# Where the down products stand among the gate and up products: the empty places move to a unit's ends, and the last five units of a half give out two columns a place

## The chip, the core and the metric

The kernel runs on one core of a Trainium2 chip. The core has TensorE (matmuls, with a queue of its own for loading weights), VectorE, ScalarE, GpSimd and SyncE, each with one queue in which instructions start in their written order; they wait for each other through semaphores. In the profile they are PE and PEld, DVE, ACT, POOL and SP. The metric is the device time of one execution in microseconds (us).

## The reference, cut to what matters

```python
def reference(x, wqkv, w_phi, wo, w_gate, w_up, w_down):
    xn = layernorm(x)                       # x is [1, 2048, 576]
    s = hedgehog_attention(xn)              # 32 heads of 18, then @ wo
    g = silu(xn @ w_gate) * (xn @ w_up)     # [2048, 4608]
    return x + s * silu(g @ w_down)         # [1, 2048, 576]
```

The inputs are float32. The change is in the FFN, the third and fourth line: gate and up projections, their gated product, and the down projection.

## The kernel before, in words

The attention takes the first 460 us or so; it also lays out `xn` and its sums as operands for the FFN. The FFN takes the rest. It treats the 2048 rows in two halves of 1024 (`i` = 0 and 1), and in each half the 4608 hidden columns in 36 blocks of 128. One block of one half is a **unit**; `n` is its place in the half, 0 to 35. Five units of half 0 and four of half 1 were computed early and are loaded from memory (`stored`); the others run `gate_up`.

`gate_up` computes gate and up of a unit by Strassen's scheme with seven products. Each is 7 matmuls of 128 x 512, accumulating into PSUM tiles `px` (two buffers), `py` and `pw` (one each). One unit runs them in this order: `px` (A11), `pw` (S1), `py` (A12), `px` again (S2), `px` (S3), `px` (A22), `pw` (S4). Between them other engines read: ScalarE copies `px` into `yp` after the first (L813), takes a snapshot `s` of `px` after the fourth and the fifth (L788), and applies silu to `py` (L800) and `px` (L804); VectorE adds snapshots to `pw` (L793) and makes the two parts of the hidden block, `ha` (L809) and `hb` (L805). The next matmul into the same tile has to wait for these readers. The order of ScalarE's queue matters too: in half 0 each unit's weights are prepared on the fly, with casts on ScalarE (L60), splits on VectorE (L61) and sums on GpSimd (L744 to L747).

The down projection is put off and cut into **items**, which are given out at the four **places** of a unit, between the products. Groups of four units (two pairs) make seven down products `p1` to `p7`, again by Strassen's scheme, of two items each, and an item costs as many columns as it has pairs: two, and 12 matmuls of 128 x 288 into a `pd` tile, of which there are two. VectorE then adds `pd` to a sum in SBUF (L1030). Units 32 and 33 are a pair alone, whose fourteen items have one column, 6 matmuls. The last two units, 34 and 35, are done plainly (`plain`): eight items of 12 matmuls, for which ScalarE first fills `pd` (or `px`, `py`, `pw`) with the sums so far (L923). Before these, the seven sums have to be combined into four (`combine`, at no cost in columns): its first part comes after `p6` in the queue (L1059 and L1060 on VectorE, L1061 on GpSimd, L1062 and L1063 on VectorE), its second after `p3` (L1067 on GpSimd, L1068 on VectorE). The second half's plain items are followed by silu, the product with the attention's rows (L903), the addition of `x` (L906) and the store (L907).

The queue's rule is `fill`, called at each place. It gives out items until it has given `share` columns (2, or 3 in the last five units, so that two two-column items go out), and stops when no more than `LAG` = 3 columns wait. A group of four units brings 28 columns for 16 places, so in steady state two of the 16 places stay empty. The operations are then ordered by a scheduling layer from priorities and readiness, which may move a later product into an empty place; the order it settles on is fixed in the program.

Of the kernel before, what the change touches and what calls it, by code (L numbers as in the profile page):

```python
# [23 lines left out]
NF = F // P  # L24
# [7 lines left out]
FIRST = (EARLY + 1, EARLY)  # L32
TAILS = (NF - EARLY + 3) // 4
LAG = 3
RUSH = NF - 5
LN_EPS = 1e-5
DEN_EPS = 1e-6

# [10 lines left out]
def gated_hedgehog_kernel(ctx: ExitStack, tc, x, w_qk, w_v, w_phi, wo, w_gu, w_tail, w_down, ident_in, mask_in, out):  # L49
# [88 lines left out]
    with ExitStack() as att:  # L138
# [17 lines left out]
        with ExitStack() as wst:  # L156
# [4 lines left out]
            with ExitStack() as pst:  # L161
# [101 lines left out]
                last, rest, _ = norm_block(2, xns[0:4])  # L263
# [508 lines left out]
    def stored(src, fill):  # L772
# [5 lines left out]
        return h  # L778

    def gate_up(w, xo, fill, opening):  # L780
        A11, A12, A22, S2, S4, S3, S1 = xo
        xp, yp, wp = (fps.tile([P, BT], F32, name=n, bufs=b) for n, b in (("px", 2), ("py", 1), ("pw", 1)))
        h = h_tile()

        def snap(ps):
            t = short("s", 3)
            with tc.high_priority():
                snaps.append(nc.scalar.copy(t, ps))  # L788
            return t

        def add(ps, t):
            with tc.high_priority():
                nc.vector.tensor_add(t, ps, t)  # L793


        if opening == 0:
            nc.tensor.matmul(yp, w[0][0][:, 0], A11[0], start=True, stop=True)

        def silu_y():
            nc.scalar.activation(yp, yp, AF.Silu)  # L800

        def silu_x(s3):
            with tc.high_priority():
                tops.append(nc.scalar.activation(xp, xp, AF.Silu))  # L804
            nc.vector.tensor_mul(h[1], xp, s3)  # L805

        def top(s2):
            with tc.high_priority():
                anchor.append(nc.vector.tensor_mul(h[0], yp, s2))  # L809

        product(xp, w, 0, A11, True, False)
        with tc.high_priority():
            copies.append(nc.scalar.copy(yp, xp))  # L813
        product(wp, w, 4, S1, True, False)
        if opening < 2:
            product(xp, w, 5, S2, False, False)
            s2 = snap(xp)
            product(yp, w, 1, A12, False, True)
            silu_y()
            product(xp, w, 2, S3, False, False)  # L820
            s3 = snap(xp)
            add(wp, s3)
            add(wp, s2)
            zp = fps.tile([P, 2, 512], F32, name="pd", bufs=2)[:, 0]
            product(zp, w, 3, S4, True, True)
            add(zp, s2)
            top(s2)
            product(xp, w, 6, A22, False, True)
            silu_x(s3)
            return h  # L830
        fill()
        product(yp, w, 1, A12, False, True)
        silu_y()
        product(xp, w, 5, S2, False, False)
        s2 = snap(xp)
        fill()
        product(xp, w, 2, S3, False, False)
        s3 = snap(xp)
        add(wp, s3)
        fill()  # L840
        product(xp, w, 6, A22, False, True)
        silu_x(s3)
        product(wp, w, 3, S4, False, True)
        add(wp, s2)
        top(s2)
        fill()
        return h
# [225 lines left out]
    for i in range(2):  # L1073
# [3 lines left out]
        for f in range(FIRST[i]):  # L1077
            order.insert(4 * f + 1 - i, f)
        units += [(i, n, f) for n, f in enumerate(order)]
    queue, anchor, share = [], [], [2]  # L1080
    copies, snaps, tops = [], [], []

    def look():
# [6 lines left out]
                step[1]()  # L1090
                step[1] = None

    def fill(lag=LAG):
        done = 0
        while queue and done < share[0] and (sum(c for q in queue for c, _ in q[2]) > lag or not queue[0][0]):
            look()
            c, item = queue[0][2].pop(0)
            item()
            done += c
            if not queue[0][2]:  # L1100
                queue.pop(0)
# [13 lines left out]
    fps = ctx.enter_context(tc.tile_pool(name="fps", bufs=1, space=PSUM, reuse_waits="tile"))  # L1115
    finals, late = {}, list(range(HT))
    for i, n, f in units:
        share[0] = 2 if n < RUSH else 3
        if i == 1 and n == 0:
            xo = operands(1)  # L1120
        if f >= FIRST[i]:
            w = kept.pop() if i and kept else ready.pop(0)
            if (i, f) == (0, NF - 1):
                kept.append(w)
            if todo and (i, f) != (0, NF - 1):
                ready.append(gate_up_weights(*todo.pop(0)))
        h = stored(h_dram[i, f], fill) if f < FIRST[i] else gate_up(w, xo, fill, f - FIRST[0] + (NF if i else 0))
        if n % 2 == 0:
            g = {"f": (f, units[units.index((i, n, f)) + 1][2]), "h": [h]}
            if n % 4 == 0:  # L1130
                group = []
            if n < NF - 2:
                group.append(g)
        else:
            g["h"].append(h)
        if n >= NF - 2:
            if n % 2:
                plain(i, g["f"], g["h"], finals)
            continue
        if n >= NF - 4 or n % 4 > 1:  # L1140
            strassen(i, group, n % 2, n < 4)
        if n % 2 == 0:
            continue
        if i and n >= 15 and late:
            with tc.issue_after(anchor[-1].ins):
                late_finish(late.pop(0))
        if n == NF - 3:
            for k in range(2):
                queue.insert(len(queue) - 2 + 3 * k,
                             [0, None, [(0, lambda i=i, k=k: combine(i, k, finals))]])  # L1150
# [37 lines left out]
```

## Time and profile before

| what | value |
|---|---|
| median of 3 runs | 1599.25 us (1598.89 to 1599.63) |
| the profiled execution's own time | 1602.31 us |
| its span, first to last instruction | 1600.40 us |
| TensorE matmuls busy | 1586.0 us |
| VectorE, ScalarE, GpSimd busy | 1172.6, 719.5, 665.5 us |
| granted TensorE clock | 0.999 |

The span is divided by engine: busy time is the sum of the instructions' durations, so an engine can be busy and still wait often for short times. A row of the timeline is one group of equal instructions, with its start, its duration, its engine and line, and in brackets how long the engine stood idle before it and what ended that. Matmuls overlap: a new 128 x 512 matmul starts about every 0.23 us though each lasts 0.39, so the distance between the starts of two groups says how long TensorE took for one.

### The profile page before, as it was taken

How to read it: one execution, taken by the hardware profiler on the slowest of the kernel's cores; microseconds unless marked ns; L12 is line 12 of the kernel's file. 1: busy time of each engine (PE TensorE's matmuls, PEld its weight loads, DVE VectorE, ACT ScalarE, POOL GpSimd, SP SyncE). 2: the span in 40 equal slices, each digit the busy share in tenths (PEclk: the TensorE clock that was granted, in tenths of full speed). 3: DMA queues.
4: the chain of work that ended last, by engine and by line, in shares of the span. 5: the costliest groups of instructions: out<-in, count | busy, mean ns of one | idle time of the engine just before them, and what ended most of it. 6: DMA issues, size and time to landing. Idle time of an engine off the chain costs nothing.

```text
span 1600.4 us, 25376 instructions
## 1 busy us (share of the span) xinstructions
PE 1586.0 (99%) x9415; PEld 1422.6 (89%) x9415; DVE 1172.6 (73%) x1729; ACT 719.5 (45%) x1400; POOL 665.5 (42%) x714
## 2 busy tenths in 40 slices
PE   8999999999999999999999999999999999999998
PEld 6899998999988888988888888888888888888887
DVE  7777769999946778887777778635667667666577
ACT  5633345445335654445444444454343333333334
POOL 2676762434115535644545435223324324133133
PEclk9999999999999999999999999999999999999999
DMA  9622243435376454555545453965545565565545
GB/s 283 219 82 80 89 147 118 120 105 144 118 247 233 165 184 165 175 180 179 179 171 194 170 190 116 333 220 148 156 138 153 183 187 159 174 181 184 144 117 178
DMA packets 123180, 268.28 MB, mean 168 GB/s; under 512 B 12978, under 2 KB 54066, under 8 KB 121778
## 3 DMA queue, kind: packets, MB, share of 16 engines
q1 hardware_dynamic: 107612, 244.73, 46.8%
q0 software_dynamic: 3552, 12.59, 2.8%
q10 hardware_dynamic: 11894, 9.35, 1.8%
q8 instruction: 74, 1.21, 0.3%
q14 instruction: 48, 0.39, 0.1%
HBM read 167.53 MB, written 99.09 MB: 167 GB/s over the span
## 4 chain that ended last, share of the span: by engine, by line
PE 94%; DVE 3%; DMA 2%; ACT 1%; issue 1%; POOL 0%; SPq 0%; ACTq 0%; DVEq 0%; POOLq 0%
PE px L759 25%; PE pd L876 25%; PE pw L759 12%; PE p L94 7%; PE py L759 6%; PE pe L94 5%; PE p L652 4%; PE kvp L330 2%; PE pt L632 2%; PE vx L418 1%; PE pt L625 1%; PE vw L418 1%; PE tp L249 1%; DMA wst<-in_A_w_qk 1%; PE vx L94 1%; PE vy L94 1%
## 5 line engine op out<-in xcount | busy, mean ns | idle before, releaser
L876 PEld LDWEIGHTS pd<-dw,hh 128*128 128x128 f32 x3012 | 424.0, 188 | 22.0 <-ACT pd L923 1.5
L876 PE MATMUL pd<-dw,hh 128*128 128x288 f32 x3012 | 438.5, 295 | 1.1 <-ACT pd L923 0.7
L759 PE MATMUL px<-X,w 128*128 128x512 f32 x1512 | 386.5, 391 | 0.0
L759 PEld LDWEIGHTS px<-X,w 128*128 128x128 f32 x1512 | 274.6, 188 | 48.9 <-ACT s L788 2.3
L759 PE MATMUL pw<-X,w 128*128 128x512 f32 x744 | 190.8, 392 | 0.0
L759 PEld LDWEIGHTS pw<-X,w 128*128 128x128 f32 x744 | 138.7, 188 | 29.4
L793 DVE TENSOR_TENSOR s<-pw,s 128x512 f32<-128x512 f32 x126 | 86.5, 688 | 97.9 <-ACT s L788 87.6
L1030 DVE TENSOR_TENSOR acc<-pd,acc 128x576 f32<-128x576 f32 x128 | 96.3, 753 | 78.9 <-PE pd L876 78.4
L788 ACT COPY s<-px 128x512 f32<-128x512 f32 x126 | 73.7, 585 | 156.6 <-PE px L759 156.6
L61 DVE TENSOR_TENSOR hh<-ha,hh 128x512 fp32r<-128x512 f32 x140 | 110.1, 812 | 22.2 <-ACT hh L60 21.5
L60 ACT CAST hh<-ha 128x512 fp32r<-128x512 f32 x140 | 82.7, 620 | 87.7 <-PE pd L876 74.3
L1002 POOL TENSOR_TENSOR hb<-hb 128x512 f32<-128x512 f32 x34 | 46.9, 1381 | 160.3 <-DVE hb L805 160.0
L94 PE MATMUL pe<-X,wh 128*128 128x512 f32 x340 | 105.6, 398 | 2.0 <-ACT wh L64 2.0
L61 DVE TENSOR_TENSOR w<-ld,w 128x512 fp32r<-128x512 f32 (+1 forms) x96 | 79.8, 832 | 35.6 <-ACT w L60 33.5
L759 PE MATMUL px<-X,wt 128*128 128x512 f32 x252 | 98.1, 389 | 0.0
L759 PE MATMUL py<-X,w 128*128 128x512 f32 x378 | 97.0, 391 | 0.0
L989 POOL TENSOR_TENSOR h<-ha,hb 128x512 f32<-128x512 f32 x34 | 44.7, 1313 | 125.1 <-DVE ha L809 94.1
L1015 POOL TENSOR_TENSOR ha<-ha 128x512 f32<-128x512 f32 x34 | 52.6, 1563 | 96.0 <-DVE hh L61 96.0
L60 ACT CAST w<-ld 128x512 fp32r<-128x512 f32 (+1 forms) x96 | 52.5, 549 | 84.8 <-POOL ld L747 55.0
L813 ACT COPY py<-px 128x512 f32<-128x512 f32 x63 | 36.0, 572 | 103.4 <-PE px L759 78.9
L744 POOL TENSOR_TENSOR ts<-ld 128x256 f32<-128x256 f32 x32 | 27.3, 855 | 122.7 <-issue 66.7
L759 PEld LDWEIGHTS py<-X,w 128*128 128x128 f32 x378 | 67.8, 188 | 10.6
(286 smaller groups left out, 3237.4 us busy)
## 6 DMA issues: line engine op xcount, KB each, us to landing
w_dram<-w SPq DMA_DIRECT2D x90, 512.0 KB
w<-w_dram SPq DMA_DIRECT2D x90, 512.0 KB
wt<-t_dram SPq DMA_DIRECT2D x62, 336.0 KB
ld<-in_B_w_gu SPq DMA_DIRECT2D x32, 512.0 KB
rt<-in_B_w_down SPq DMA_DIRECT2D x33, 288.0 KB
rb<-in_B_w_down SPq DMA_DIRECT2D x33, 288.0 KB
w_dram<-w SPq DMA_DIRECT2D x30, 256.0 KB
w<-w_dram SPq DMA_DIRECT2D x30, 256.0 KB
```

The costliest lines, as they stand in the source:

```text
L60: nc.scalar.copy(hi, src)
L61: nc.vector.tensor_sub(lo, src, hi)
L94: last = nc.tensor.matmul(ps, l, r, start=n == 0, stop=n == len(pairs) - 1)
L652: nc.tensor.matmul(ps[:, 0:HALF], a[0:w, g, jc], bw[0:w, g, n], start=k == 0, stop=k == 3 * NG - 1)
L759: nc.tensor.matmul(ps, l, r, start=first and n == 0, stop=last and n == len(mm) - 1, skip_group_check=True)
L788: snaps.append(nc.scalar.copy(t, ps))
L793: nc.vector.tensor_add(t, ps, t)
L876: nc.tensor.matmul(ps, l, r, start=first and n == 0 and m == 0, stop=n == len(hs) - 1 and m == 2, skip_group_check=True)
L989: sub(s, g["h"][0][0], g["h"][0][1])
L1002: nc.gpsimd.tensor_add(a21, a21, g["h"][1][1])
L1015: sub(a12, a12, g["h"][0][0])
L1030: nc.vector.tensor_add(a2, pd[:, :, 0:HALF], a2)
```

## The change

What `fill` gives out at each place changes in three ways. A unit's first place is left empty when no more than 6 columns wait (`2 * LAG`), unless it is the last unit of a half. The share is 2 columns at all places but those of unit 34, where it is 3; in unit 35 the lag is 0, so that it gives out all that is left. And an item that costs nothing (a part of `combine`) is given out as soon as it is at the head of the queue.

```diff
-RUSH = NF - 5
 def gate_up(w, xo, fill, opening):
...
-        fill()
+        if waiting() > 2 * LAG or not rush[1]:
+            fill()
         product(yp, w, 1, A12, False, True)
...
-    queue, anchor, share = [], [], [2]
+    queue, anchor, rush = [], [], [2, LAG]
...
+    def waiting():
+        return sum(c for q in queue for c, _ in q[2])
+
-    def fill(lag=LAG):
+    def fill(lag=None):
+        lag = rush[1] if lag is None else lag
         done = 0
-        while queue and done < share[0] and (sum(c for q in queue for c, _ in q[2]) > lag or not queue[0][0]):
+        while queue and (not queue[0][0] or done < rush[0] and waiting() > lag):
             look()
...
     for i, n, f in units:
-        share[0] = 2 if n < RUSH else 3
+        rush[:] = 3 if n == NF - 2 else 2, 0 if n == NF - 1 else LAG
```

Columns given out at the four places, worked out from the two rules, where they differ:

| unit | before | after |
|---|---|---|
| 22, 26, 30 of half 0; 18, 22, 26, 30 of half 1 | 2 2 0 0 | 0 2 2 0 |
| 2 of half 1 | 2 2 0 0 | 0 2 0 0 |
| 31 of both | 4 4 0 0 | 2 2 2 2 |
| 32 of both | 4 4 4 4 | 2 2 2 2 |
| 33 of both | 4 3 0 0 | 2 2 2 2 |
| 34 of both | 3 3 3 1 | 4 3 3 3 |
| 35 of both | 0 0 0 0, three left over | 2 2 2 1 |
| 0 of half 1 (stored, two places) | 2 3 | 2 2 |

The changed program's line numbers are one lower from L36 to L830 (so L813 becomes L812) and the same from L832 to L1080. Three places of the program follow, as the scheduling layer ordered them.

TensorE in unit 22 of half 0, from its first product, before:

```order
L759 MATMUL px<-X_60,w_8156 128x512 x6
L759 MATMUL px<-X_60,wt_5183 128x512
L759 MATMUL pw<-X_5202,w_8165 128x512 x6
L759 MATMUL pw<-X_5202,wt_5183 128x512
L876 MATMUL pd<-dw,hh 128x288 x12
L759 MATMUL py<-X_61,w_8156 128x512 x6
L759 MATMUL py<-X_61,wt_5183 128x512
L759 MATMUL px<-X_5207,w_8165 128x512 x6
L759 MATMUL px<-X_5207,wt_5183 128x512
L876 MATMUL pd<-dw,hh 128x288 x12
```

and in the change:

```order
L758 MATMUL px<-X_60,w_8156 128x512 x6
L758 MATMUL px<-X_60,wt_5183 128x512
L758 MATMUL pw<-X_5202,w_8165 128x512 x6
L758 MATMUL pw<-X_5202,wt_5183 128x512
L758 MATMUL py<-X_61,w_8156 128x512 x6
L758 MATMUL py<-X_61,wt_5183 128x512
L758 MATMUL px<-X_5207,w_8165 128x512 x6
L758 MATMUL px<-X_5207,wt_5183 128x512
L876 MATMUL pd<-dw,hh 128x288 x12
L758 MATMUL px<-X_5212,w_8169 128x512 x6
L758 MATMUL px<-X_5212,wt_5183 128x512
L876 MATMUL pd<-dw,hh 128x288 x12
```

The item between `pw` and `py` is gone; one stands after the fifth product instead.

ScalarE at the same place, in the change (`w2` and `w1` are the next unit's weights, `ld` and `ts` their raw parts and sums from GpSimd, `py_8347` is this unit's `yp`):

```order
L59 CAST w2_8325<-ld_8322 128x2x256
L59 CAST w1_8342<-ld_8322 128x256
L812 COPY py_8347<-px_8346 128x512
L59 CAST w2_8334<-ts_8324 128x2x256
L799 ACTIVATE py_8347<-py_8347 128x512
```

The first three rows stand as they did before; only the rows behind them moved (the casts of the next items' `hh` and `dw`, which stood behind the copy, now follow `py`'s silu).

VectorE in the last unit of half 1, from L1059 on, before (`pd_15853`, `pd_15861` and `pd_15869` are the last three one-column items, of `p2` and `p3`; `s`, `hb` and `ha` belong to units 34 and 35):

```order
L1059 TENSOR_TENSOR X02_11072<-X02_11072 128x1152
L793 TENSOR_TENSOR s_15656<-pw_15583,s_15656 128x512
L805 TENSOR_TENSOR hb_15585<-px_15581,s_15702 128x512
L809 TENSOR_TENSOR ha_15584<-py_15582,s_15656 128x512
L1060 TENSOR_TENSOR sx_11129<-sx_11129,X02_11072 128x1152
L1030 TENSOR_TENSOR acc_5181<-pd_15765,acc_5181 128x576
L1062 TENSOR_TENSOR acc_5181<-sx_11129,acc_5181 128x1152
L1063 TENSOR_TENSOR acc_5181<-acc_5181,sx_11129 128x1152
L61 TENSOR_TENSOR hh_15847<-hb_15585,hh_15847 128x512
L1030 TENSOR_TENSOR acc_5181<-pd_15853,acc_5181 128x576
L61 TENSOR_TENSOR dw_15844<-ld_15838,dw_15844 128x576
L793 TENSOR_TENSOR s_15817<-pw_15775,s_15817 128x512
```

and in the change (`pd_15802` and `pd_15820` are the items of `p2`, `pd_15828` and `pd_15854` those of `p3`; `s`, `ha` and `hb` belong to unit 35):

```order
L1059 TENSOR_TENSOR X02_11072<-X02_11072 128x1152
L1030 TENSOR_TENSOR acc_5181<-pd_15802,acc_5181 128x576
L792 TENSOR_TENSOR s_15817<-pw_15725,s_15817 128x512
L1060 TENSOR_TENSOR sx_11129<-sx_11129,X02_11072 128x1152
L1030 TENSOR_TENSOR acc_5181<-pd_15820,acc_5181 128x576
L1062 TENSOR_TENSOR acc_5181<-sx_11129,acc_5181 128x1152
L792 TENSOR_TENSOR s_15781<-pw_15725,s_15781 128x512
L1063 TENSOR_TENSOR acc_5181<-acc_5181,sx_11129 128x1152
L808 TENSOR_TENSOR ha_15726<-py_15724,s_15781 128x512
L1030 TENSOR_TENSOR acc_5181<-pd_15828,acc_5181 128x576
L804 TENSOR_TENSOR hb_15727<-px_15723,s_15817 128x512
L1030 TENSOR_TENSOR acc_5181<-pd_15854,acc_5181 128x576
```

Before, L1059 stood among the last results of unit 34; now it stands in the middle of unit 35, behind the add of `p6`'s second item. After the rows shown come, in both programs, the rest of what the plain items need: in the change the split of a weight (`dw_15876`), L1068 and the low part of a hidden block (`hh_15882`), in this order. The end of half 0 has the same rows in the same order; there TensorE has `px`, `pw`, `py`, `px` of unit 1 of half 1 ahead of the plain items.

## The prediction

> **What bounds the kernel now.** I read the page first, then busy time by stretches of 50 us, then the waits of TensorE's two queues, then the timeline where they lie.
>
> From the page: busy time by engine, and the chain that ended last.
>
> ```profile
> PE 1586.0 (99%) x9415; PEld 1422.6 (89%) x9415; DVE 1172.6 (73%) x1729; ACT 719.5 (45%) x1400; POOL 665.5 (42%) x714
> PE 94%; DVE 3%; DMA 2%; ACT 1%; issue 1%; POOL 0%; SPq 0%; ACTq 0%; DVEq 0%; POOLq 0%
> ```
>
> TensorE is the bound: the change neither adds nor removes a matmul, so it can only move the time in which TensorE waits. What there is to win is small, as the stretches (PE, PEld, DVE, ACT, POOL busy) and the load queue's waits (total, times, longest) show:
>
> ```profile
> 750.00:800.00 50.00, 50.00 (x271) 43.79 (x270) 39.07 (x55) 24.02 (x49) 26.54 (x26) 1.00 0.50 175
> 1550.00:1600.00 50.00, 43.35 (x258) 38.61 (x256) 38.05 (x53) 22.90 (x45) 17.62 (x13) 0.99 0.51 174
> ...
> PEld px L759 <- ACT s L788: 2.3, 12, 0.2
> PEld pd L876 <- ACT pd L923: 1.5, 3, 0.7
> PEld pd L876 <- DVE X L1030: 1.0, 2, 0.8
> PEld pd L876 <- DVE acc L1030: 0.9, 4, 0.3
> ```
>
> The first wait is the one the change is about: `xp` may be written again only when ScalarE's `snap` has read it, and a place left empty there has no matmuls to cover that. The other three are waits for a `pd` bank, in the last five units and the tail. Together 2.3 + 1.5 + 1.0 + 0.9 = 5.7 us: the most the change can win in the FFN.
>
> The prices I use are in the timeline. First, unit 22 of half 0 and the same place of units 26 and 30:
>
> ```profile
> 781.20 0.39 PE L759 MATMUL pw<-X,wt 128*128 128x512 f32 x1
> 781.31 0.75 POOL L747 TENSOR_TENSOR ld<-ld,ts 128x256 f32<-128x256 f32 x1
> 781.42 1.75 PE L876 MATMUL pd<-dw,hh 128*128 128x288 f32 x12
> 782.09 0.41 ACT L60 CAST w<-ld 128x256 fp32r<-128x256 f32 x1 [4.83 <-POOL ld L747]
> 782.40 0.58 ACT L813 COPY py<-px 128x512 f32<-128x512 f32 x1
> 783.03 1.63 PE L759 MATMUL py<-X,w 128*128 128x512 f32 x6
> 784.73 1.52 PE L759 MATMUL px<-X,w 128*128 128x512 f32 x6
> 786.32 1.75 PE L876 MATMUL pd<-dw,hh 128*128 128x288 f32 x12
> ...
> 849.43 0.58 ACT L813 COPY py<-px 128x512 f32<-128x512 f32 x1
> 850.07 1.67 PE L759 MATMUL py<-X,w 128*128 128x512 f32 x6
> ...
> 916.49 0.58 ACT L813 COPY py<-px 128x512 f32<-128x512 f32 x1
> 917.12 1.65 PE L759 MATMUL py<-X,w 128*128 128x512 f32 x6
> ```
>
> (Columns: start, duration, engine and instruction, then the idle time before it and what ended it.) A product of 7 matmuls takes 786.32 - 784.73 = 1.59 us, a two-column item of 12 about 1.58. A wait that the cover nearly hides costs the six matmuls 1.63 instead of 1.52: 0.1 us.
>
> The tail of half 1:
>
> ```profile
> 1555.57 1.75 PE L876 MATMUL pd<-dw,hh 128*128 128x288 f32 x12
> 1556.57 1.55 DVE L1030 TENSOR_TENSOR acc<-pd,acc 128x576 f32<-128x576 f32 x2 [1.43 <-PE pd L876]
> ...
> 1568.83 2.67 POOL L1061 TENSOR_TENSOR X<-X,acc 128x1152 f32<-128x1152 f32 x1 [12.25 <-DVE sx L1060]
> 1569.33 3.38 DVE L1062 TENSOR_TENSOR acc<-sx,acc 128x1152 f32<-128x1152 f32 x1
> 1572.64 1.34 DVE L1063 TENSOR_TENSOR acc<-acc,sx 128x1152 f32<-128x1152 f32 x1
> 1573.91 0.68 DVE L61 TENSOR_TENSOR hh<-hb,hh 128x512 fp32r<-128x512 f32 x1
> 1574.51 0.74 DVE L1030 TENSOR_TENSOR acc<-pd,acc 128x576 f32<-128x576 f32 x1
> 1575.17 0.74 DVE L61 TENSOR_TENSOR dw<-ld,dw 128x576 fp32r<-128x576 f32 x1
> 1575.33 3.11 POOL L1067 TENSOR_TENSOR acc<-acc,X 128x1152 f32<-128x1152 f32 x1 [3.83 <-DVE acc L1030]
> 1575.84 0.68 DVE L793 TENSOR_TENSOR s<-pw,s 128x512 f32<-128x512 f32 x1
> 1576.44 0.74 DVE L1030 TENSOR_TENSOR acc<-pd,acc 128x576 f32<-128x576 f32 x1
> ...
> 1579.57 0.64 ACT L923 COPY pd<-acc 128x576 f32<-128x576 f32 x1
> 1580.26 1.86 PE L876 MATMUL pd<-dw,hh 128*128 128x288 f32 x12 [0.21 <-ACT pd L923]
> 1582.58 1.86 PE L876 MATMUL pd<-dw,hh 128*128 128x288 f32 x12 [0.46 <-ACT pd L923]
> 1582.97 1.35 DVE L1068 TENSOR_TENSOR acc<-acc,X 128x1152 f32<-128x1152 f32 x1
> 1585.87 3.37 PE L876 MATMUL pd<-dw,hh 128*128 128x288 f32 x24
> 1589.07 1.75 PE L876 MATMUL px<-dw,hh 128*128 128x288 f32 x12
> ```
>
> From start to start, VectorE's costs are 0.66 for an add out of `pd`, 0.67 for a wide split, 0.60 for an add out of `pw` or a narrow split, 1.27 for a 1152-wide add; a down matmul is (1589.07 - 1585.87) / 24 = 0.133. An add can start 1.0 us after its one-pair item's first matmul (1555.57, 1556.57). GpSimd's and VectorE's adds inside SBUF exclude each other: L1062 ended 1.21 after L1061 did, 3.38 long where L1063 took 1.34. L1067 began beside the split of 1575.17 and ended 2.53 after it: 2.55 alone. Adds with an operand in PSUM (1575.84, 1576.44) ran beside it at full speed.
>
> **The change, part by part.** *Waits that go.* Of the 5.7 us I take 4.5 as won (a 0.19 wait of the load queue holds the matmuls for only about 0.1), between 2 and 5.7. New bank waits come where three one-column items meet two banks, in units 34 and 35: some four per half at 0.1 to 0.25, 1.1 in all.
>
> *The first place of units 22, 26 and 30 of half 0.* Without the item, `py` follows `pw` directly and must wait for the copy L813 into `yp`. In half 0 that copy stands in ScalarE's queue behind the cast of `w1`, which waited 4.83 us for GpSimd's L747; the order of both queues up to there is unchanged. TensorE would be ready at 781.42, the copy ends at 782.98, and `py` can start at 783.03, as before: 1.6 us idle. What hid it was the item, which now comes later and costs its 1.58 again. The other two units show the same copy and the same `py`. 3 x 1.58 = 4.75. If GpSimd's chain were short this would be 0. In half 1 no such cast stands ahead, so I cost it at nothing there: the cover is the product `pw`, 1.59 against a 0.58 copy.
>
> *The last unit of a half: later combine.* Before, unit 34 gave out all but three columns, and the first combine ran under unit 35. Now unit 35 gives out 7, and the combine cannot begin before the second item of `p6`. I count from the unit's first matmul, with no waits on TensorE: `p6`'s item starts at 8.75, the last item, `p3`'s, at 16.70, and the plain items could start at 17.50. VectorE's queue after that `p6` item, in the order of the changed program: add 9.75 to 10.41, split 11.08, L1059 12.35, add 13.01, `wp` add 13.61, L1060 14.88, add 15.54. GpSimd's L1061 runs 14.95 to 17.62, so L1062 ends at 18.83. GpSimd's L1067 no longer waits for `p2` and follows at once, to 21.4; VectorE's `wp` add runs beside it, but L1063 has to wait: 22.6. Then `ha` 23.2, the add that frees the bank of the first plain item 23.85, `hb` 24.45, add 25.1, split 25.8, L1068 27.05, and the low part of `hh` that the plain items need 27.75.
>
> At the end of half 1 TensorE does 10 plain matmuls (written ahead as 3 + 2 + 3 + 2) and then stands until 27.8, where without waits it would have reached that point at 17.50 + 10 x 0.133 = 18.83: 9.0 us. ScalarE's silu now stands ahead of the next bank's filling: 0.5 more. The remaining 86 matmuls and the output follow as before.
>
> The combine also issues loads: its rows for the final product go out on SyncE, in the order they had, as soon as the last unit has read `X00` and `X13` for the last time (2.4 and 4.0); their first reader is the multiplication after 27.8, so they cost nothing. If they were the last thing needed, they would add their landing time to the tail; with over 20 us between I leave that out. The next half's operand loads have 15 us from 2.4 to 17.50 for the first, in place of the six products and three one-pair items between them before (6 x 1.59 + 3 x 0.8 = 11.9).
>
> At the end of half 0 four products of the next half stand before the plain items. `pw` waits for the `wp` add (19.55 against 19.09): 0.45. `py` needs `yp`, which `ha`, queued behind L1063, still reads: 23.3, copy 23.9, against 21.14: 2.8. The plain items then find L1068 and its filling ready at 27.8, as TensorE arrives. Sum 3.3.
>
> Sum: -4.5 + 1.1 + 4.75 + 3.3 + 9.5 = +14.1. The profiled execution took 1602.31 for a span of 1600.40; the median of the runs is 1599.25, 3.06 below, and I add the sum to that: **1613.4 us**.
>
> Bounds: if L1063 got through ahead of L1067, it would end at 20.65, and both half ends shrink by 1.95: +10.2. If the copies too were in time: +5.5. Upward, L1062 losing to L1067 first or the wins being 2: +17.
>
> The Trainium skill's page SBUF — State Buffer, section "Who interferes with whom", says that a VectorE instruction with two SBUF inputs and a GpSimd instruction that reads SBUF exclude each other for the whole instruction, by issue order. It speaks against this change, and the trace agrees (3.38 against 1.34); by it L1063 waits for L1067, as in my sum.
>
> **The rivals.** (a) *The places do what they are for, and the half ends hide themselves*: faster, 1599.25 - 4.5 + 1.1 = 1595.9. For it: VectorE is only 38 of 50 us busy at the end. Against it: its idle time lies before the `p6` item, and the queue after it is in a fixed order. (b) *The waits only change place*: early stalls of 4.75 against 4.5 won, with both combines covered: 1599.25 - 4.5 + 1.1 + 4.75 = 1600.6, no change. It needs VectorE to reach L1068 by 17.5, when 17.3 us of work start at 9.75. (c) *The copies are in time, the combine is not*: 1599.25 + 14.1 - 4.75 = 1608.6. Decided at `py` of unit 22: if GpSimd's L747 ends 1.6 us earlier, no wait. (d) *No exclusion between L1063 and L1067*: 1599.25 + 10.2 = 1609.5.
>
> **How the numbers follow.** My forecast, slower by the combine and the copies, 0.60; (c) 0.13, (d) 0.13, (b) 0.07, (a) 0.07. The likeliest gives 1613.4. (c) and (d) belong in the range, the low end, 1605, is (c) and (d) together (1599.25 + 5.5 = 1604.7), the high end, 1617, the upper bound; what is left out is mostly (a) and (b). A change of 0.2%, 3.2 us, is about what can be told from none: slower needs over 1602.4, that is my forecast, (c), (d) and a little of (b), 0.87; within 0.08; faster 0.05.
>
> **What would show it.** The waits of TensorE's queues would gain `py` behind ACT L813 (three of 1.6 us near 781, 849 and 917), and `pd` behind VectorE and ACT L923 of some 9 us after 1585. L1063 would take over 3 us instead of 1.34. DVE should show no idle time in the last unit after its `p6` item. The waits of `px` for L788 should fall well below 2.3. I am wrong if L1068 starts within 2 us of the last `p3` item's end, or if `py` follows `pw` without a gap in units 22, 26 and 30.

## The result and the profile after

The changed kernel takes 1611.95 us (median of 4 runs, 1611.73 to 1613.29), the kernel before on the same chip 1599.44 (1598.89 to 1600.91): ratio 1.0077, 95% interval 1.0064 to 1.009. It is slower by 12.5 us; the forecast was 1613.4.

The profiled execution took 1611.96 us for a span of 1610.2. These rows of its page and of TensorE's waits (total, times, longest) answer to those of before; the last is a group row, which ends with the idle time ahead of the group and what ended most of it:

```profile
PE 1584.5 (98%) x9415; PEld 1423.4 (88%) x9415; DVE 1168.3 (73%) x1729; ACT 718.9 (45%) x1400; POOL 664.9 (41%) x714
PE py L758 <- ACT py L812: 6.8, 4, 2.5
PE pd L876 <- ACT pd L923: 6.8, 1, 6.8
L758 PEld LDWEIGHTS px<-X,w 128*128 128x128 f32 x1512 | 274.4, 188 | 45.6 <-ACT s L787 0.2
```

TensorE is as busy as before. The wait of `py` is new, and the one for a `pd` bank behind ScalarE's L923 has grown from 0.7 us to 6.8. The load queue's wait for the snapshot, which the change is about, is down from 2.3 to 0.2 us.

**The first place of unit 22**, on the timeline (start, duration, instruction, idle time before it and what ended that); units 26 and 30 show the same:

```profile
778.39 0.72 POOL L746 TENSOR_TENSOR ld<-ld,ts 128x256 f32<-128x256 f32 x1
779.14 0.40 ACT L59 CAST w<-ld 128x256 fp32r<-128x256 f32 x1 [4.82 <-POOL ld L746]
779.46 0.58 ACT L812 COPY py<-px 128x512 f32<-128x512 f32 x1
780.09 1.67 PE L758 MATMUL py<-X,w 128*128 128x512 f32 x6 [1.44 <-ACT py L812]
```

`py` stands ready behind `pw`, and ScalarE's copy is late because the cast ahead of it waits for GpSimd's sum. From matmul to matmul the three gaps are 1.60 us longer than usual each (at 778.26, 846.67 and 915.05).

**The last unit of half 1**, from its `p6` item on. Its first matmul starts at 1562.77:

```profile
1572.51 0.76 DVE L1030 TENSOR_TENSOR X<-pd,X 128x576 f32<-128x576 f32 x1 [2.37 <-PE pd L876]
...
1577.91 2.68 POOL L1061 TENSOR_TENSOR X<-X,acc 128x1152 f32<-128x1152 f32 x1 [14.63 <-DVE sx L1060]
1578.42 3.38 DVE L1062 TENSOR_TENSOR acc<-sx,acc 128x1152 f32<-128x1152 f32 x1
1580.55 3.72 POOL L1067 TENSOR_TENSOR acc<-acc,X 128x1152 f32<-128x1152 f32 x1
1582.33 3.16 DVE L1063 TENSOR_TENSOR acc<-acc,sx 128x1152 f32<-128x1152 f32 x1
1586.01 0.74 DVE L1030 TENSOR_TENSOR acc<-pd,acc 128x576 f32<-128x576 f32 x1
1586.79 0.64 ACT L923 COPY pd<-acc 128x576 f32<-128x576 f32 x1 [7.91 <-DVE acc L1030]
1587.48 6.85 PE L876 MATMUL pd<-dw,hh 128*128 128x288 f32 x24 [6.82 <-ACT pd L923]
1588.60 1.35 DVE L1068 TENSOR_TENSOR acc<-acc,X 128x1152 f32<-128x1152 f32 x1
1589.87 0.68 DVE L60 TENSOR_TENSOR hh<-hb,hh 128x512 fp32r<-128x512 f32 x1
1594.13 1.87 PE L876 MATMUL px<-dw,hh 128*128 128x288 f32 x12
```

The VectorE queue is full from 1572.5 on, L1062 and L1063 both take over 3 us beside GpSimd's L1061 and L1067, and the bank for the first plain item becomes free behind them. TensorE stands for 6.98 us. Then 24 plain matmuls take 1594.13 - 1587.48 = 6.65 us, twice the 24 x 0.133 = 3.2 of before. The windows say why for the most part (busy time of PE, PEld, DVE, ACT and POOL, then the granted clock, DMA share and GB/s):

```profile
1580.00:1585.00 5.00, 0.66 (x5) 0.42 (x4) 5.00 (x3) 0.00 (x0) 4.27 (x2) 0.91 0.62 223
1585.00:1590.00 5.00, 2.52 (x8) 2.15 (x9) 5.00 (x8) 2.83 (x5) 0.00 (x0) 0.50 0.00 0
1590.00:1592.00 2.00, 2.00 (x9) 1.73 (x9) 1.75 (x3) 0.00 (x0) 0.00 (x0) 0.50 0.04 8
1592.00:1594.00 2.00, 2.00 (x10) 2.00 (x10) 0.58 (x1) 1.25 (x3) 0.00 (x0) 0.50 0.00 0
1594.00:1596.00 2.00, 2.00 (x16) 2.00 (x15) 0.97 (x3) 1.53 (x4) 1.49 (x2) 0.91 0.00 0
```

The granted clock is at half from 1584.13 to 1594.37, that is 10.24 us. At half clock a matmul of 288 columns starts every 0.24 us, which makes 24 x 0.24 = 5.8 of the 6.65; the rest are short waits, the longest of them in the load queue, 0.28 us for a weight's split and 0.27 for `hh`.

**Where the time went.** I add up, for the FFN's matmuls, how much further apart their starts lie than the usual 0.2265 us (512 columns) and 0.132 (288), and compare the sums of the two profiles. From the first product to the last matmul the FFN takes 1110.84 us before and 1123.75 after, 12.9 more:

| stretch | before | after | difference |
|---|---|---|---|
| the three waits of `py`, half 0 | 0 | 4.8 | +4.8 |
| wait of `pw` and `py` at the end of half 0 | 0 | 3.05 | +3.05 |
| from 1550 on, the end of half 1 | 2.0 | 11.0 | +9.0 |
| all other short waits | 7.4 | 3.4 | -4.0 |

The profiled times themselves differ by less, 1611.96 - 1602.31 = 9.65, because the attention in the profiled execution of before happened to end 2.9 us later (its first FFN product is at 482.88, after at 479.94); the medians differ by 12.5.

### The profile page after: what moved, and what is told of

It reads as the page before. It is cut to its first block, busy times and chain, and to the rows that moved or that the text cites. A ratio compares the mean times of both kernels' runs of the same rounds, so it can differ in the third digit from the quotient of the medians.

```text
span 1610.2 us, 25367 instructions
## 1 busy us (share of the span) xinstructions
PE 1584.5 (98%) x9415; PEld 1423.4 (88%) x9415; DVE 1168.3 (73%) x1729; ACT 718.9 (45%) x1400; POOL 664.9 (41%) x714
## 5 line engine op out<-in xcount | busy, mean ns | idle before, releaser
L812 ACT COPY py<-px 128x512 f32<-128x512 f32 x63 | 36.1, 572 | 108.0 <-PE px L758 97.1
```

## The experiments

Twelve kernels. All start from the changed kernel, and each diff is against it, but for the last, which is against the kernel ahead of it. The kernel before took 1599.6 to 1600.1 us beside them; ratios are against it, with their 95% intervals.

### The first place empty in half 1 alone

```diff
-        if waiting() > 2 * LAG or not rush[1]:
+        if waiting() > 2 * LAG or not rush[1] or opening < NF:
```

> The changed kernel, but the first place is left empty in half 1 alone; in half 0 the first place gives out as before. Theory (in half 0 the copy into yp stands in ScalarE's queue behind a cast that waits for GpSimd): the three waits of py of 1.6 us each go, and the waits for the snapshot that they had replaced come back (0.2 in each of the three units), so 1611.95 - 3 x 1.71 + 0.66 = 1607.5. Rival (everything is lost at the ends of the halves, py's waits are made good later): 1612, with the waits gone and the ends later by as much.

Measured: 1608.37 us (1607.99 to 1609.13), ratio 1.0053 (1.0036 to 1.007). The three waits of 1.60 are gone; the wait at the end of half 0 (0.41 + 2.68) and that at the end of half 1 (6.99, with 10.24 us of half clock) are unchanged. The loss in units 22, 26 and 30 belongs to the empty place of half 0; it is worth 3.6 us by the medians, about one less than the 4.8 of the waits.

### The shares of the last five units as before

```diff
-        rush[:] = 3 if n == NF - 2 else 2, 0 if n == NF - 1 else LAG
+        rush[:] = 2 if n < NF - 5 else 3, LAG
```

> The changed kernel with the old rule for the last five units (up to three columns a place, three columns left over at the end of a half); the empty first places stay. Theory (the ends of the halves lose by the late combine, some 9 us and 3 us less what the old ends waited for banks): only the copies' waits stay, 1599.44 + 4.5 - 0.45 = 1603.5, and L1063 takes 1.34 again. Rival (the empty first places are what delays VectorE, and with it the ends): it stays over 1608.

Measured: 1603.93 us (1603.23 to 1605.45), ratio 1.0025 (1.0016 to 1.0035). Eight of the 12.5 us hang on the share rule. TensorE's waits in the FFN, as far as they are new against before:

```profile
PE py L758 <- ACT py L812: 4.3, 3, 1.4
PE px L758 <- ACT s L787: 1.2, 1, 1.2
PE pd L876 <- DVE acc L1030: 0.4, 1, 0.4
```

The three of `py` stay. The second row, at 1574.92 in unit 35, neither before nor the changed kernel has; it costs 1.38 us from start to start and is taken up below. The third, for an item's bank at the end of half 0 (1016.94), costs 0.5 us and comes up there too. The clock stays at 1.00.

### The shares of before in half 1 alone

```diff
-        rush[:] = 3 if n == NF - 2 else 2, 0 if n == NF - 1 else LAG
+        rush[:] = (2 if n < NF - 5 else 3, LAG) if i else (3 if n == NF - 2 else 2, 0 if n == NF - 1 else LAG)
```

> The changed kernel with the share rule of before in the last five units of half 1 alone; half 0 keeps the new shares, and the first place stays empty in both halves. Theory (the end of half 1 carries most of the loss): the waits above 1550 fall from 11.0 to 3.6 us as in the run with old ends, those near 780, 847, 915 and at half 0's end stay: 1611.95 - 7.4 = 1604.6 us, and the clock stays at 1.00 up to the end. Rival (the end of half 0 is worth as much, through what it delays in half 1): 1607 or more.

Measured: 1605.73 us (1604.85 to 1607.84), ratio 1.004 (1.0026 to 1.0054). The 7.4 us expected came to 6.2 by the medians, and to 7.3 in the traces, where the FFN takes 1116.42 us in place of 1123.75; the 1604.6 of the theory is a ratio of 1.003, inside the interval. The waits of half 0 all stay (`py` behind L812: 6.8 us, 4 times, as in the changed kernel), the clock stays at 1.00. So the end of half 1 is the largest part of the loss, and what happens at the end of half 0 does not travel on to it.

### Three columns from unit 33 on

A try at a better rule: the last five units still without three columns over, but faster at first, so that the combine should come earlier. The first place is empty in half 1 alone.

```diff
-        if waiting() > 2 * LAG or not rush[1]:
+        if waiting() > 2 * LAG or not rush[1] or opening < NF:
-        rush[:] = 3 if n == NF - 2 else 2, 0 if n == NF - 1 else LAG
+        rush[:] = 3 if n >= NF - 3 and n < NF - 1 else 2, 0 if n == NF - 1 else LAG
```

> Empty first places in half 1 alone, and three columns a place in units 33 and 34 instead of 34 alone, so that p6 is out before the last unit begins, while units 31 and 32 give two a place and unit 35 gives out the rest. Theory (it is the late combine that costs, not two columns a place): the combine lies under unit 35 as in the kernel before, no wait over 1 us is left at either end, and the waits for banks in units 31 to 33 stay gone: 1599.44 - 1.5 (half 0's end) - 0.7 - 0.45 = 1596.8. Rival (two columns a place push too much into the last two units, whatever the combine): 1605 or more.

Measured: 1604.94 us (1603.95 to 1606.84), ratio 1.0033 (1.0022 to 1.0045). A miss by 8 us. The largest wait of TensorE, two rows of the timeline at the end of half 0, and two windows there:

```profile
PE pd L876 <- DVE acc L1030: 5.0, 3, 3.0
...
1006.26 2.66 POOL L1061 TENSOR_TENSOR X<-X,acc 128x1152 f32<-128x1152 f32 x1
1008.95 1.36 DVE L1063 TENSOR_TENSOR acc<-acc,sx 128x1152 f32<-128x1152 f32 x1 [3.32 <-POOL X L1061]
...
1012.00:1014.00 2.00, 2.00 (x10) 1.71 (x9) 2.00 (x4) 0.00 (x0) 1.68 (x1) 0.66 0.13 55
1014.00:1016.00 2.00, 2.00 (x9) 1.81 (x9) 2.00 (x2) 0.75 (x2) 1.41 (x1) 0.50 0.45 82
```

The combine does come early, but then GpSimd, which is still preparing weights for the last items, reaches L1061 late, and L1063, which writes what L1061 reads, holds VectorE idle for 3.32 us with the adds of one-column items queued behind it. TensorE waits 3.14 us at 1008.27 for a bank and then has the clock at half for 3.4 us. In half 1 the same adds cost 1.80 us at 1571.67, and gaps of 1.0 and 0.6 follow. In this kernel as in the changed one, items of unit 35 collide with the combine on VectorE; before has three items there, and the adds of all three come behind L1062. That any place of the combine among them would cost as much is not shown.

### Unread matmuls in the gap at the end

28 matmuls of 128 x 512 behind the last `p3` item, into a tile that nothing reads, to keep TensorE busy through the 7 us.

```diff
+    warm = fps.tile([P, BT], F32, name="px", bufs=2)
+    for _ in range(28):
+        nc.tensor.matmul(warm, w[0][3][:, 0], xo[4][0], start=True, stop=True, skip_group_check=True)
     while queue:
         fill(0)
```

> The changed kernel with 28 matmuls of 128 x 512 (6.3 us) that nobody reads, put on TensorE in its wait at the end of half 1, behind the last one-column item. VectorE's order is the same; TensorE's plain items are no longer written ahead in pieces. Theory (the granted clock falls to half after the wait, and the first plain matmuls run at 0.24 us each instead of 0.132): the clock stays full, from 1590.55 on the remaining 19 of the first 24 plain matmuls take 0.132 each, and the 24 end 1.1 us earlier: 1610.9. Rival (the slow matmuls follow VectorE's results, not the clock): 1612, with the same 0.24 spacing at full clock.

Measured: 1613.44 us (1612.52 to 1615.12), ratio 1.0084 (1.0069 to 1.0099): no gain. TensorE's timeline and the windows:

```profile
1580.99 6.52 PE L1157 MATMUL px<-X,w 128*128 128x512 f32 x28
1588.04 0.97 PE L876 MATMUL pd<-dw,hh 128*128 128x288 f32 x4 [0.54 <-ACT pd L923]
1589.29 0.40 PE L876 MATMUL pd<-dw,hh 128*128 128x288 f32 x1 [0.28 <-DVE dw L60]
1591.16 4.32 PE L876 MATMUL pd<-dw,hh 128*128 128x288 f32 x19 [1.48 <-DVE hh L60]
...
1585.00:1590.00 5.00, 3.87 (x17) 2.53 (x15) 5.00 (x7) 2.66 (x5) 0.00 (x0) 1.00 0.00 0
1590.00:1592.00 2.00, 0.84 (x5) 0.84 (x6) 2.00 (x4) 0.17 (x1) 0.00 (x0) 0.91 0.00 0
1592.00:1594.00 2.00, 2.00 (x10) 2.00 (x10) 0.70 (x2) 1.05 (x3) 0.00 (x0) 0.50 0.00 0
```

The clock stays at 1.00 through the gap, and the first four plain matmuls come 0.13 us apart; but TensorE then waits 0.55, for a weight's split, and 1.74, for the low part of `hh`, and the clock falls to half from 1591.62 to 1595.03, 3.41 us. So the slow matmuls are a matter of the granted clock, and the expected gain did not come because the sparse stretch behind the padding was enough to lose it again. That the 24 matmuls with a clock at full would have ended earlier was not shown.

### The cast ahead of the copy on GpSimd

In half 0 the high half of `w1` is cast on GpSimd, whose sum it waits for, and no longer on ScalarE. The first place stays empty in both halves.

```diff
-                split(w[:, :, 0:2], w[:, :, 2:4], src)
+                if m == 6 and i == 0:
+                    nc.gpsimd.tensor_copy(w[:, :, 0:2], src)
+                    nc.vector.tensor_sub(w[:, :, 2:4], src, w[:, :, 0:2])
+                else:
+                    split(w[:, :, 0:2], w[:, :, 2:4], src)
```

> The changed kernel, with one thing other: the high half of w1 (the seventh weight product of a unit, made of a GpSimd difference at line 747) is cast on GpSimd instead of ScalarE in half 0, so that ScalarE has nothing ahead of the copies at lines 812 and 813 that waits for GpSimd. The place of the down items stays empty in both halves. Theory (the three 1.60 us waits of py in units 22, 26 and 30 come because the copy at 812 stands behind a cast that waits for GpSimd): the three waits go, the ends stay as they are (2.7 us in half 0, 7 us and the half clock in half 1), 1611.95 - 3 x 1.6 = 1607.2 us. Rival (the copies are late because the adds before them, or ScalarE's own load, are late): the three waits stay and the time is 1612.

Measured: 1611.49 us (1608.76 to 1613.01), ratio 1.007 (1.0057 to 1.0084). The time misses the theory by 4 us, while the trace bears out its mechanism. In unit 22 (lines behind the edit are four higher: L816 is the copy of L812; the view's window ends within the third row, after four of its six matmuls):

```profile
780.56 1.52 PE L762 MATMUL pw<-X,w 128*128 128x512 f32 x6
780.85 0.57 ACT L816 COPY py<-px 128x512 f32<-128x512 f32 x1 [2.86 <-DVE ha L812]
782.15 1.07 PE L762 MATMUL py<-X,w 128*128 128x512 f32 x4
...
PE pd L880 <- DVE hh L60: 1.5, 1, 1.5
...
1020.00:1025.00 5.00, 2.50 (x10) 1.68 (x9) 5.00 (x6) 1.94 (x4) 1.16 (x1) 0.93 1.02 430
1025.00:1030.00 5.00, 5.00 (x20) 4.12 (x19) 4.38 (x7) 2.47 (x5) 0.60 (x1) 0.73 0.86 295
```

The copy now runs beside `pw`, and `py` follows without a gap, in all three units. The 4.8 us were spent elsewhere. At the start of the FFN, where GpSimd is behind, new gaps of 0.6 and 1.6 us open near 507, before items whose `hh` is late (the row with `hh` is the second), and one of 0.4 near 495. And the wait at the end of half 0, as long as in the changed kernel (2.67 against 2.68), this time is followed by 3.4 us of half clock, where seven matmuls come 0.43 apart in place of 0.23: 1.4 us. -4.8 + 2.6 + 1.4 is -0.8. In the traces the FFN is 2.2 us shorter than in the changed kernel, because there is one more difference: after the 6.98 us wait at the end of half 1, as long as in the changed kernel, the clock stays at half for 6.83 us and not for 10.24, which is worth 1.0, and short waits are 0.4 less. The medians say -0.5, with single runs from 1608.76 to 1613.01.

### The sum of C11 on VectorE

```diff
-            nc.gpsimd.tensor_add(C11, C11, P1)
             nc.vector.tensor_add(C12, C12, P6)
+            nc.vector.tensor_add(C11, C11, P1)
```

> The changed kernel, with one thing other: in the combination of the seven products, the sum of C11 with P1 at line 1067 is made on VectorE behind line 1068 instead of on GpSimd, so that GpSimd has no operation of this group beside VectorE's line 1063. Theory (a VectorE add takes 3.2 us instead of 1.35 when GpSimd works on SBUF at the same time): line 1063 takes 1.35 us at both ends, line 1068 the same, the moved sum 1.35 behind them; the 2.68 us wait at the end of half 0 falls below 1.5, the wait at the end of half 1 becomes about 0.5 us shorter; 1609 to 1610.5 us. Rival (the long adds are a matter of their operands): line 1063 still takes 3.2 us, each end is longer by the 1.35 of the moved sum where it stands ahead of the last copies, 1613 to 1614.5 us.

Measured: 1610.92 us (1609.53 to 1612.03), ratio 1.0069 (1.0054 to 1.0085); against the changed kernel a difference of 1.0, which the intervals don't separate. The trace decides. End of half 1:

```profile
1577.07 2.68 POOL L1061 TENSOR_TENSOR X<-X,acc 128x1152 f32<-128x1152 f32 x1 [14.63 <-DVE sx L1060]
1577.58 3.38 DVE L1062 TENSOR_TENSOR acc<-sx,acc 128x1152 f32<-128x1152 f32 x1
1581.48 1.34 DVE L1063 TENSOR_TENSOR acc<-acc,sx 128x1152 f32<-128x1152 f32 x1
1586.54 1.35 DVE L1067 TENSOR_TENSOR acc<-acc,X 128x1152 f32<-128x1152 f32 x1
```

L1062, still beside GpSimd's L1061, takes its 3.38 us; L1063, now alone, 1.34 in place of 3.16, with the same operands. The same is seen at the end of half 0, where `py`'s wait falls from 2.68 to 0.80. At the end of half 1 the moved sum gives most of it back, as expected: the FFN is 1121.10 us long, 2.65 less, 1.9 of it at half 0.

### Half 1 alone, with the shares of before

Both of the first two edits: only the first place of half 1 and the loop of `fill` are left of the change.

```diff
-        if waiting() > 2 * LAG or not rush[1]:
+        if waiting() > 2 * LAG or not rush[1] or opening < NF:
-        rush[:] = 3 if n == NF - 2 else 2, 0 if n == NF - 1 else LAG
+        rush[:] = 2 if n < NF - 5 else 3, LAG
```

> The kernel before with the empty first place in half 1 alone: the share rule of the last five units is that of before, and in half 0 the first place is filled as before. Theory (the three waits of 1.60 and the two ends are all that the change costs): 1603.93 of the run with the old ends, less 3 x 1.6, plus the 0.66 of short waits that before had in the units of half 0: 1599.8; against before a gain of at most the 0.45 us of short waits in half 1, 1599.0 to 1600. Rival (the empty place in half 1 is itself worth more, since the many waits under 0.06 us shrink with it): 1597 to 1598.5. Other rival: the 1.39 us wait that the run with the old ends showed in front of unit 35's last products comes from the empty place and stays, 1601.

Measured: 1600.85 us (1599.85 to 1602.51), ratio 1.0007 (0.9998 to 1.0016). The time and the wait are those of the third expectation: the 1.38 us wait near 1570 stays. The short waits of half 1 ahead of the last five units do fall, by 1.1 us, but this wait and the one of 0.5 at the end of half 0 (1012.09) cost more. That the wait comes from the empty place, as the expectation has it, does not follow; later kernels speak to that.

### The same with the last five units left out

```diff
-        if waiting() > 2 * LAG or not rush[1]:
+        if waiting() > 2 * LAG or rush[0] > 2 or opening < NF:
-        rush[:] = 3 if n == NF - 2 else 2, 0 if n == NF - 1 else LAG
+        rush[:] = 2 if n < NF - 5 else 3, LAG
```

> The empty first place in half 1 alone, and there only ahead of its last five units; all else, the share rule too, as in the kernel before. Theory (the 1.38 us wait near 1570 of the run with old ends came from empty places in the last five units): that wait is gone, the short waits of half 1 are about 0.06 us in a stretch of 50: 1600.85 - 1.38 = 1599.5 less 0 to 1, 1598.5 to 1599.5. Rival: the wait stays, 1600.8.

Measured: 1601.02 us (1599.71 to 1601.77), ratio 1.0006 (0.9997 to 1.0015). A miss: the wait stays, so empty first places in the last units do not make it.

### Both halves, the cast on GpSimd, the shares of before

The diffs of the cast and of the shares together.

> The empty first place in both halves, the share rule of the last five units as before, and the high half of w1 of half 0 cast on GpSimd. Theory (waits behind the cast, and the ends, are all that the change costs): 1603.93 - 3 x 1.6 = 1599.1 us, the kernel before within 0.2%. Rival (the cast on GpSimd delays GpSimd's differences, which feed the next products): 1601 or more. Rival (empty first places are worth the 4.5 us that the prediction gave them once both costs are gone): 1595 to 1597.

Measured: 1602.13 us (1601.13 to 1603.98), ratio 1.0016 (1.0007 to 1.0025): the first rival. No wait of `py` is left, but the delay of `hh` near 507 is there (0.6 + 1.6 us), this time with a stretch of half clock behind it (508.96, 3.41 us), and so are the 1.38 near 1573 and the 0.5 at the end of half 0. What comes late is above all the `hh` of items; only 0.4 us, near 494, stand before a product, which is what the rival named.

### The places mended

Empty first places ahead of the last five units only, in both halves; the cast on GpSimd from the fifth gate and up tile on; the shares of before.

```diff
-                split(w[:, :, 0:2], w[:, :, 2:4], src)
+                if m == 6 and i == 0 and f - FIRST[0] > 3:
+                    nc.gpsimd.tensor_copy(w[:, :, 0:2], src)
+                    nc.vector.tensor_sub(w[:, :, 2:4], src, w[:, :, 0:2])
+                else:
+                    split(w[:, :, 0:2], w[:, :, 2:4], src)
-        if waiting() > 2 * LAG or not rush[1]:
+        if waiting() > 2 * LAG or rush[0] > 2:
-        rush[:] = 3 if n == NF - 2 else 2, 0 if n == NF - 1 else LAG
+        rush[:] = 2 if n < NF - 5 else 3, LAG
```

> The empty first place in the units ahead of the last five of each half alone; in the last five the first place is filled and the share rule is that of before; the high half of w1 of half 0 is cast on GpSimd from the fifth gate and up tile on (the first four stay on ScalarE, since the run with this cast everywhere waited 2.1 us for hh near 507). Theory (empty first places remove the short waits, and the three 1.60 us waits, the ends and the GpSimd cast in the first units were all that they cost): the FFN loses the about 1.6 us of short waits that before has between 750 and 950 and the about 2.4 between 1050 and 1550: 1599.6 - 4 = 1595.6 us, 1595 to 1597. Rival (what is left waiting goes into the last five units and comes back there, as the 1.38 us wait near 1570 did in the runs with old ends): 1597.5 to 1599. Rival (no gain that can be measured): 1599 to 1600.5.

Measured: 1598.35 us (1597.76 to 1600.61), ratio 0.9992 (0.9983 to 1.0): the first rival. The waits near 507 and the three of `py` are gone; the 1.38 is left. It reads, in unit 35 (L1066 and L1067 are the changed kernel's L1062 and L1063):

```profile
1567.29 1.34 DVE L1067 TENSOR_TENSOR acc<-acc,sx 128x1152 f32<-128x1152 f32 x1
1568.56 0.68 DVE L808 TENSOR_TENSOR hb<-px,s 128x512 f32<-128x512 f32 x1
1569.27 0.62 ACT L59 CAST hh<-hb 128x512 fp32r<-128x512 f32 x1 [1.82 <-DVE hb L808]
1569.80 0.58 ACT L791 COPY s<-px 128x512 f32<-128x512 f32 x1
1570.43 1.66 PE L762 MATMUL px<-X,w 128*128 128x512 f32 x6 [1.21 <-ACT s L791]
...
1008.98 1.36 DVE L1067 TENSOR_TENSOR acc<-acc,sx 128x1152 f32<-128x1152 f32 x1 [3.32 <-POOL X L1065]
```

The snapshot stands behind the cast of an `hh`, the cast behind `hb`, and `hb` behind the combine. Before, `hb` stands ahead of L1060 and its cast ends at 1566.92 + 0.62 = 1567.54. The likely mover of the combine is the third part of the change, the loop that gives out an item without columns at once; the next kernel tests it. The last row is the end of half 0: the combine stands early there too, VectorE waits 3.32 us for GpSimd's part, and an item's bank comes free late, which costs TensorE 0.5 us (at 1010.94).

### And the loop of before

```diff
-        while queue and (not queue[0][0] or done < rush[0] and waiting() > lag):
+        while queue and done < rush[0] and (waiting() > lag or not queue[0][0]):
```

on top of the last kernel.

> As places_mended, and the loop that gives items out is that of before as well: an item without columns (the combination of the seven products) has to wait for a place that has columns left to give, where the change gives it out at once. Apart from this the two kernels are one. By this the combination of half 1 stands in unit 35 where before has it, behind the second sums of px and py, and not ahead of them. Theory (the 1.38 us wait near 1570, where px waits for ScalarE's copy of the snapshot, ScalarE for the cast of hh and that for VectorE's 4.8 us of lines 1062 and 1063, comes from this alone): that wait is gone, the others as in places_mended: 1598.35 - 1.38 = 1597.0 us, 1596.4 to 1597.6, faster than before beyond doubt. Rival (the wait comes from the other number of columns that waits at that point): it stays, 1598.3. Rival (it goes but comes back at the last products or the plain items): 1598 to 1599.

Measured: 1596.87 us (1595.98 to 1598.14), ratio 0.998 (0.9971 to 0.9989): faster than the kernel before by 3.2 us, and as forecast. The same place:

```profile
1567.15 0.59 ACT L791 COPY s<-px 128x512 f32<-128x512 f32 x1 [1.00 <-PE px L762]
1567.80 1.66 PE L762 MATMUL px<-X,w 128*128 128x512 f32 x6
...
PE pd L880 <- ACT pd L927: 0.7, 2, 0.5
PE pd L880 <- DVE X L1034: 0.5, 1, 0.5
```

These are the only waits that the view lists for the matmuls of this FFN; both the 1.38 and the 0.5 are gone, so both came from the loop. The FFN is 1108.54 us long against the 1110.84 of before.

## Why the prediction was right, and where it was not

**The sum.** Predicted +14.1, measured +12.9 in the FFN and +12.5 in the medians. Its terms:

| term | predicted | measured |
|---|---|---|
| waits that go, less new bank waits | -4.5 + 1.1 | about -4.0 up to 1550, and the 2.0 of before's own end |
| units 22, 26 and 30 of half 0 | +4.75 | +4.8 |
| end of half 0 | +3.3 | +3.05 |
| end of half 1 | +9.5 | +11.0 |

- **Units 22, 26 and 30**: right in size and cause. The cause is shown by moving the cast, after which `py` follows `pw` without a gap. When the place is filled again in half 0, the FFN gets only 4.2 us shorter in the traces (3.6 by the medians), since about 0.8 us of short waits of half 0 come back.
- **VectorE's queue in the last unit**: the low part of `hh` was to be there 27.75 us after the unit's first matmul; it ends at 1589.87 + 0.68 = 1590.55, which is 27.78. L1062 was to end at 18.83 and ends at 19.03, L1063 at 22.6 and ends at 22.7.
- **The exclusion of L1063 and L1067**: right. L1063 takes 3.16 us, and 1.34 where GpSimd's sum is moved away. The rule of the Trainium skill that the prediction drew on agrees with both numbers. Rival (d) is out, and so are (a), (b) and (c), by the waits.
- **End of half 0**: 0.37 + 2.68 against 0.45 + 2.8, in the order foreseen.
- **The step that was mis-sized is the end of half 1**, 9.5 against 11.0. The prediction let TensorE do ten plain matmuls at full speed before it stands, and had the rest follow as before. It stands ahead of the first one (the bank's add, which the prediction itself put 23.85 after the unit's start, ends at 1586.75, 23.98), and ten of the 24 matmuls come before `hh`, at half clock. The eleventh starts 27.84 after the unit's first, as foreseen (27.8). The other fourteen, from 1590.61 to 1594.13, take 3.52 us in place of 14 x 0.133 = 1.86: 1.7 us that no step had. What failed is the term for the matmuls behind the wait, put at nothing more than before. Without these 1.7 the end is 9.3, and that this is near 9.5 is in part luck: the 0.5 for ScalarE's silu ahead of the next bank's filling is not found (no gap over 0.06 us behind 1594.37), and other short gaps add up to about as much.
- **The waits that go** were 2.6 us more than the net -3.4: -4.0, and -2.0 that counts against the end. Part of the reason is the term for new bank waits: 1.1 predicted, about 0.25 found. The rest are gaps under 0.06 us, which no row of waits shows and the prediction did not count; they fell from 3.9 to 2.2, by 1.7. The 5.7 us that it called the most the change can win was too low: the short waits fell by 6.0. This error and the one at the end of half 1 have opposite signs, so that the total is closer than its terms is luck.
- **A step that was missing**: the loop that gives out the combine at once was described and got no price. In the changed kernel the combine is late anyway; with the shares of before it costs 1.5 us by the medians (1598.35 against 1596.87), by the traces 1.38 in unit 35 and 0.5 at the end of half 0.

That the empty first place is worth having where no copy is late and the ends are those of before is shown for half 1: of the 2.3 us by which the last kernel's FFN is shorter than that of before (3.2 by the medians), 1.3 lie there, and there the two kernels differ in the empty first places alone. In half 0, where the other 1.0 lies, the cast is moved as well, and no kernel has the cast alone; that filling the places again brought 0.8 us of short waits back speaks for the places there too. In the changed kernel they stood against 4.8 us of late copies and 12 at the two ends.

## What to carry to other kernels

Before work is moved out from in front of a wait, look at what the engine that ends that wait has ahead of the releasing instruction: here an idle time of 4.8 us in ScalarE's queue, harmless behind an item, showed at once when the item left. At the end of a stage the last results should be spread so that the engine which collects them gets its long operations while the bound engine still has other work; a queue that is emptied evenly to the last place leaves all of it for after. And an edit that removes a proven wait may not show in the time, as the cast did not: compare the waits of the two traces, stretch by stretch, before the theory is dropped.

## What the hardware did that was not expected

TensorE's granted clock fell to half after gaps of some microseconds, and the time it stayed there came in pieces of 3.41 us: 10.24 (three pieces) after the 6.98 us wait of the changed kernel, 6.83 (two) after the same wait in the kernel with the cast on GpSimd, 6.83 in the run with C11 on VectorE, 3.41 in the padded run and in three others. The Trainium skill, page TensorE: Matmul & The Clock Gate, Part 1, says that the clock is decided by a free-running window of about 3.4 us, down to half after an idle one and up again after a busy one. The pieces agree.

Within a run the steps of the clock lie on one grid: in the kernel with the cast on GpSimd it fell at 1024.33 and at 1584.12, and the 559.79 us between are 164 x 3.4133. So the same wait may or may not cost it, by where it lies on the grid, and that is seen at the end of half 0. In the changed kernel a border at 1024.34 cuts the 2.7 us wait in two; matmuls were busy for 1.81 us of the piece before the border, and the clock stayed at 1.00. With the cast on GpSimd the wait lies within one piece, 1020.92 to 1024.33, with matmuls busy for 0.91 us, and cost 3.41 us of half clock.

That piece was not idle, and neither was the one of the padded run: between 1588.21 and 1591.62 matmuls were busy for 1.66 us, and the clock fell all the same. Laid over the traces of all fourteen kernels, the grid puts the line near half a piece: at full clock no piece with 1.80 us or more of matmul time was followed by half clock, every piece with 1.5 or less was, and between 1.56 and 1.75 it went either way. The profile models when a matmul ends, so these busy times are rough.
